# Two tiles for the turned reciprocals, and a new order table for the attention stage

## The chip, the cores and the metric

The kernel is written by hand for one core of one Trainium2 chip. The metric is the time of one execution on the device, in microseconds (us). The engines that the text names are TensorE (PE, with its weight loads shown apart as PEld), VectorE (DVE), ScalarE (ACT), GpSimd (POOL) and SyncE (SP, which here only issues transfers).

## The reference

The program runs cluster attention, then a channel mix, then a token and channel mixer, on 2 batches of 768 positions with 512 features (8 heads of 64), all in float32. Cut to what matters:

```python
# attention, per batch and head: S = 768, D = 64, 16 clusters
q_assign = argmax(q_n @ c_n.T)          # cluster of each query, the same for keys
mask     = q_assign[:, None] == k_assign[None, :]
scores   = where(mask, (q @ k.T) / 8, -1e9)
attn     = exp(scores - rowmax(scores))
out      = (attn / (rowsum(attn) + 1e-9)) @ v
# channel mix: xk, xr are mixes of x with x shifted by one position
x = sigmoid(xr @ w_r) * (relu(xk @ w_k) ** 2 @ w_v)
# mixer
u = x + (relu(x.T @ w_tok1) @ w_tok2).T
out = u + relu(u @ w_ch1) @ w_ch2
```

## The kernel before, in words

**The attention stage** works on 8 pairs, a pair being two heads of one batch. A pair has 12 tasks: two halves of the queries (hf 0 and 1), three blocks of 128 query rows in a half, and the two heads. For a task PE makes the scores (L688, 8 matmuls), DVE takes the row maxima (L696), and ACT takes the exponential from PSUM (L705) and sums its rows on the way. For hf 0 PE turns the tile (L755, two groups of three matmuls), and DVE (L460) or ACT (L462) copies each group to SBUF as ptp. For hf 1 DVE turns 32x32 blocks (L734, into the tile tb), and after the sixth task 16 transfers "ptd<-tb" (L744, 11 issued by SP, 5 by POOL) move the blocks into place. Then PE multiplies by the values (L771, 12 matmuls for a half), and DVE scales the result by the reciprocal row sums and writes it to xT (L780).

**The reciprocals** go a way of their own, once for each half: POOL adds 1e-9 (L711), DVE takes the reciprocal into the tile rsp (L714) and turns it into the tile rst (L717), SP saves rst to DRAM (L721, "rrow<-rst"), and two loads bring it back as one row broadcast over the partitions, rb (L728). There is one rsp and one rst, so the next half's turn waits until the save has read rst.

**The work of the next pair** runs beside this: ACT and POOL split q and k into a high and a low part (L462, L464, L509), PE takes the similarities to the cluster centres (L518, L563), DVE finds the best centre (L568 to L585), and from that a mask is made (L609, L614, L621). Also beside it run five conversions of 128x512 weights into high and low parts (`w_split`): a shift on DVE (L287), two more DVE operations (L291, L297), a comparison (L305), two copies on ACT and a subtraction (L311 on DVE, or on POOL for the gate's weights). At the end the shifted mixes of x for the gate are made (L382, L384, L391, L393), and PE runs 18 gate steps (54 matmuls of L439) between the values' products of the last pairs.

**The order** of all this is not found at run time. Every step above is an `Op` with an engine, a planned duration and what it depends on, and a table of 1141 numbers, `ORDER`, written into the source, says in which order the ops are issued; each engine then runs its own in that order. `ON_VECTOR` says which copies of turned tiles are DVE's, `BANKS` which PSUM bank an op uses. The planner that made the table has a clock for each engine, and a lock for what it counts as using both DVE and POOL at the port that they share: ops marked `two=True` don't overlap there. After the stage comes the dense part (L1159, L1197 and following), whose order is made while the program is built.

Of the kernel before, what the change touches and what calls it, by code (L numbers as in the profile page):

```python
# [9 lines left out]
F32 = mybir.dt.float32  # L10
# [8 lines left out]
P = 128  # L19
# [77 lines left out]
)  # L97
ON_VECTOR = {
    30, 37, 46, 148, 155, 157, 164, 171, 282, 289, 294, 296, 426, 435, 551, 678, 692, 699, 704, 815, 822, 831, 939, 946, 960, 962,
}  # L100
BANKS = (
    "6650647526504652105640246012402641432063254310476306320462046042630254376541063403642020460476307625"
    "6417024704676024024026471602165405264750742062042754065276410632043263204204604260235426543054365406"
    "525062076436720634721064012607654320"
# [26 lines left out]
def cluster_attention_moe_mixer(ctx: ExitStack, tc, q, k, v, cent, mu_k, mu_r, w_k, w_v, w_r, w1, w2, wc1, wc2, out):  # L131
    nc = tc.nc
# [313 lines left out]
    with ExitStack() as actx:  # L446
        vp = actx.enter_context(tc.tile_pool(name="vp", bufs=2))
        ep = actx.enter_context(tc.tile_pool(name="ep", bufs=4))
        ptp = actx.enter_context(tc.tile_pool(name="ptp", bufs=1))
        sml = actx.enter_context(tc.tile_pool(name="sml", bufs=2))  # L450
        dram = actx.enter_context(tc.tile_pool(name="dram", bufs=2, space=bass.MemoryType.DRAM))
        rsp = sml.tile([P, 32], F32, tag="rsp", bufs=1, name="rsp")
        rst = sml.tile([P, 32], F32, tag="rst", bufs=1, name="rst")

        pairs = [(b, p) for b in range(B) for p in range(NPAIR)]
        raws, stks, vts = {}, {}, {}

        def copy(eng, dst, src):
            if eng == "D":
# [1217 lines left out]
```

## Time and profile before

| | |
|---|---|
| median of 3 runs | 603.25 us (603.0 to 604.57) |
| the profiled execution, its own time | 603.43 us |
| span of the profiled execution | 601.6 us |
| PE busy | 591.5 us (98%), 3273 matmuls |
| PE weight loads busy | 489.7 us (81%) |
| DVE busy | 505.2 us (84%), 952 instructions |
| ACT busy | 352.5 us (59%) |
| POOL busy | 129.7 us (22%) |
| granted TensorE clock | 1.00 |

The span is what the trace covers; the execution's own time is 1.8 us longer. Times of single instructions below count from the start of the span. The attention stage fills about the first 218 us of it, the dense part the rest.

### The profile page before, as it was taken

How to read it: one execution, taken by the hardware profiler on the slowest of the kernel's cores; microseconds unless marked ns; L12 is line 12 of the kernel's file. 1: busy time of each engine (PE TensorE's matmuls, PEld its weight loads, DVE VectorE, ACT ScalarE, POOL GpSimd, SP SyncE). 2: the span in 40 equal slices, each digit the busy share in tenths (PEclk: the TensorE clock that was granted, in tenths of full speed). 3: DMA queues.
4: the chain of work that ended last, by engine and by line, in shares of the span. 5: the costliest groups of instructions: out<-in, count | busy, mean ns of one | idle time of the engine just before them, and what ended most of it. 6: DMA issues, size and time to landing. Idle time of an engine off the chain costs nothing.

```text
span 601.6 us, 9577 instructions
## 1 busy us (share of the span) xinstructions
PE 591.5 (98%) x3273; PEld 489.7 (81%) x3273; DVE 505.2 (84%) x952; ACT 352.5 (59%) x661; POOL 129.7 (22%) x182
## 2 busy tenths in 40 slices
PE   8999999999999999999999999999999999999997
PEld 6666767757667668999999998889999998998896
DVE  5999999999999779999579888989889867766634
ACT  4998988988878767967566566134343332222210
POOL 4554644744441750000000000220220000000000
PEclk9999999999999999999999999999999999999999
DMA  8278869888647542343204457245543003233002
GB/s 285 87 207 230 207 199 239 213 266 243 183 133 207 136 155 71 134 127 126 70 2 141 134 184 277 77 133 176 159 122 106 1 1 109 92 124 131 1 0 106
DMA packets 42160, 84.09 MB, mean 140 GB/s; under 512 B 9280, under 2 KB 23104, under 8 KB 42112
## 3 DMA queue, kind: packets, MB, share of 16 engines
q1 hardware_dynamic: 39168, 76.01, 41.3%
q0 software_dynamic: 2944, 7.48, 5.0%
q8 instruction: 26, 0.43, 0.3%
q14 instruction: 22, 0.18, 0.1%
HBM read 51.42 MB, written 8.65 MB: 100 GB/s over the span
## 4 chain that ended last, share of the span: by engine, by line
PE 87%; DVE 7%; issue 2%; DMA 2%; SPq 1%; ACT 1%; POOL 0%; DVEq 0%; POOLq 0%
PE ps L1159 19%; PE ps L1197 18%; PE ps L771 8%; PE ps L1467 8%; PE ps L688 8%; PE ps L1479 7%; PE ps L439 6%; PE ps L755 3%; DVE junk L696 3%; PE ps L1341 3%; PE ps L1253 3%; DVE tb L734 1%; DMA t<-k_dram 1%; SPq L744 1%; PE ps L790 1%
## 5 line engine op out<-in xcount | busy, mean ns | idle before, releaser
L1197 PE MATMUL ps<-wu,hl 128*128 128x512 f32 x486 | 115.2, 391 | 0.0
L1197 PEld LDWEIGHTS ps<-wu,hl 128*128 128x128 f32 x486 | 90.9, 188 | 18.0
L705 ACT ACTIVATE e<-ps,nm 128x768 f32<-128x768 f32 x96 | 86.4, 901 | 15.4 <-DVE junk L696 12.4
L696 DVE TENSOR_SCALAR_CACHE_REDUCE junk<-ps 128x768 bf16<-128x768 f32 x96 | 90.6, 944 | 3.3 <-DVE junk L696 0.9
L1159 PE MATMUL ps<-xmix,wu 128*128 128x384 f32 x384 | 69.2, 335 | 0.0
L1159 PEld LDWEIGHTS ps<-xmix,wu 128*128 128x128 f32 x384 | 67.3, 188 | 1.1
L309 ACT ACTIVATE wu<-g 128x512 fp32r<-128x512 f32 x52 | 32.7, 628 | 47.4 <-DVE g L305 47.2
L1300 POOL DMA_DIRECT2D uperm<-ublk x32 | 16.0, 507 | 203.2 <-DVE ublk L1279 171.6
L688 PE MATMUL ps<-ka,qa 128*128 128x384 f32 x192 | 55.5, 370 | 0.6 <-DVE ptp L460 0.2
L1467 PE MATMUL ps<-wu,hl 128*128 128x512 f32 x216 | 54.7, 393 | 0.0
L1159 PE MATMUL ps<-ut,wu 128*128 128x384 f32 x288 | 52.0, 335 | 0.0
L1159 PEld LDWEIGHTS ps<-ut,wu 128*128 128x128 f32 x288 | 50.5, 188 | 0.9
L688 PE MATMUL ps<-kb,qb 80*128 80x384 f32 x192 | 49.7, 340 | 1.0 <-DVE qb L632 1.0
L1467 PEld LDWEIGHTS ps<-wu,hl 128*128 128x128 f32 x216 | 40.2, 188 | 6.7
L734 DVE STREAM_TRANSPOSE tb<-e 128x768 f32<-128x768 f32 x48 | 44.6, 957 | 0.8 <-DMA t<-q_dram 0.7
L1526 ACT ACTIVATE hl<-t 128x384 fp32r<-128x384 f32 x24 | 12.6, 525 | 55.7 <-DVE t L1522 55.7
L688 PEld LDWEIGHTS ps<-ka,qa 128*128 128x128 f32 x192 | 30.9, 189 | 13.9 <-ACT e L705 6.7
L305 DVE SCALAR_TENSOR_TENSOR g<-wu,g 128x512 f32<-128x512 f32 x52 | 38.7, 746 | 3.9
L1522 DVE TENSOR_TENSOR t<-ps,t 128x384 f32<-128x384 f32 x42 | 22.9, 556 | 22.1 <-PE ps L1479 21.8
L755 PE MATMUL ps<-ident,e 128*128 128x128 f32 x288 | 38.9, 274 | 1.9 <-ACT e L705 1.1
L311 DVE TENSOR_TENSOR wu<-g,wu 128x512 fp32r<-128x512 f32 x48 | 33.1, 690 | 6.4 <-ACT wu L309 5.0
L755 PEld LDWEIGHTS ps<-ident,e 128*128 128x128 f32 x288 | 33.2, 141 | 6.1 <-ACT e L705 1.6
(144 smaller groups left out, 1091.4 us busy)
## 6 DMA issues: line engine op xcount, KB each, us to landing
ptd<-tb SPq DMA_DIRECT2D x88, 144.0 KB, 4.0
wraw<-moe_w_ch_dram SPq DMA_DIRECT2D x24, 512.0 KB, 3.6
t<-q_dram SPq DMA_DIRECT2D x16, 384.0 KB, 4.9
t<-k_dram SPq DMA_DIRECT2D x16, 384.0 KB, 4.5
ptd<-tb POOLq DMA_DIRECT2D x40, 144.0 KB, 4.5
spill<-wu SPq DMA_DIRECT2D x10, 512.0 KB, 3.0
wu<-spill SPq DMA_DIRECT2D x10, 512.0 KB, 4.0
wraw<-moe_w_k_dram SPq DMA_DIRECT2D x9, 512.0 KB, 5.8
```

The source lines that it names most:

```text
L305: nc.vector.scalar_tensor_tensor(out=gf, in0=f32(t[:, 1, :]), scalar=TINY, in1=gf, op0=ALU.is_ge, op1=ALU.mult)
L439: nc.tensor.matmul(gps[b, st][1], xr(xl, c, slice(st * P, (st + 1) * P)), u[:, wl, :], start=(c == 0 and n == 0), stop=(c == KD - 1 and n ...
L688: nc.tensor.matmul(ps[:, nh, 0:HS], x[:, e, c0 : c0 + P], y[:, e, nh * HS : (nh + 1) * HS], start=first, stop=not first,)
L696: nc.vector.tensor_scalar(junk, PS_[t][:, :, 0:HS], -SCALE, None, op0=ALU.mult, op1=ALU.min, accum_out=nm)
L705: nc.scalar.activation(et.rearrange("p (a b) -> p a b", a=2), PS_.pop(t)[:, :, 0:HS], AF.Exp, bias=NM_.pop(t), scale=SCALE, accum_out=ss_[ ...
L734: nc.vector.transpose(out=T_[n][:, :, e, :, i, :].rearrange("p j k q -> p k j q"), in_=E_.pop(t).rearrange("p (k j c) -> p k j c", j=4, c=32),
L755: nc.tensor.transpose(ps[:, kk], E_[t][:, kt * P : (kt + 1) * P], ident)
L771: nc.tensor.matmul(o, vts[n][:, e, kt, :], m, start=(kt == 0), stop=(kt == NT - 1))
L1159: nc.tensor.matmul(ps[:, 0:HS], u[:, wl, c, :], xin(xl, c, sl), start=(n == 0), stop=(n == 11))
L1197: nc.tensor.matmul(accs[st], prev[:, xl, st * P : (st + 1) * P], u[:, wl, :], start=(idx == 1 and n == 0), stop=(idx == nf and n == 2),)
L1467: nc.tensor.matmul(accs[st], self.hl[q][k][:, xl, st * P : (st + 1) * P], u[:, wl, :], start=(left[st] == 2 * np_ - 1 and n == 0), stop=(l ...
L1479: nc.tensor.matmul(ps[:, 0:HS], a(wl, c), b(xl, c), start=(n == 0), stop=(n == 5))
```

## The change

It has three parts. First, a second tile for the turned reciprocals: the halves hf 0 go on using rst, the halves hf 1 use the first 32 columns of csq, a small tile of the start of the program that is now allocated earlier. The rules of the plan follow: a reciprocal comes after the last turn (rsp free) and no longer after the last save, and a turn comes after the save before last. Second, the first step of a weight conversion, the shift, is marked as using the shared port, as the four DVE steps behind it were already. Third, `ORDER`, `ON_VECTOR` (26 entries in both) and `BANKS` are found anew with that.

```diff
-    9, 10, 18, 17, 1051, 1059, 1067, 2, 0, 1, 19, 26, 124, 20, 16, 3, 21, 4, 5, 27, 22, 24, 33, 23, 6, 28, 7, 8, 34, 14, 25, 11, 15, 29, 31, 12, 35,
...
+    9, 10, 18, 17, 1051, 1059, 1067, 2, 0, 1, 19, 26, 124, 20, 16, 3, 21, 27, 4, 22, 28, 24, 5, 33, 6, 25, 7, 29, 1052, 14, 34, 30, 11, 15, 12, 35,
...
-        rst = sml.tile([P, 32], F32, tag="rst", bufs=1, name="rst")
+        csq = sml.tile([P, D], F32, tag="csq", bufs=1, name="csq")
+        rsts = [sml.tile([P, 32], F32, tag="rst", bufs=1, name="rst"), csq[:, 0:32]]
...
         def rturn(n, hf):
-            nc.vector.transpose(out=rst, in_=rsp)
+            nc.vector.transpose(out=rsts[hf], in_=rsp)
...
-            nc.sync.dma_start(out=d.rearrange("r (j q) -> j r q", j=4), in_=rst)
+            nc.sync.dma_start(out=d.rearrange("r (j q) -> j r q", j=4), in_=rsts[hf])
...
-        csq = sml.tile([P, D], F32, tag="csq", bufs=1, name="csq")
...
-            o = rec_[n, hf] = Op("D", 0.12, lambda: recip(n, hf), [o] + list(row_.values())[-1:])
-            o = Op("D", 0.15, lambda: rturn(n, hf), [o])
+            o = rec_[n, hf] = Op("D", 0.12, lambda: recip(n, hf), [o] + rturns[-1:])
+            o = Op("D", 0.15, lambda: rturn(n, hf), [o] + list(row_.values())[-2:-1])
+            rturns.append(o)
```

In the changed kernel the line numbers are one higher from L453 on and two higher behind the attention stage.

**DVE, where the fourth conversion's shift (L287) stood.** This is the preparation of pair 6, which runs beside pair 5's scores; xT_98 holds the second batch's attention output. Before:

```order
L696 TENSOR_SCALAR junk,nm<-ps 128x768
L571 TENSOR_TENSOR ps<-ps,mx 128x384
L576 TENSOR_TENSOR ps<-ps,rank 128x384
L287 TENSOR_SCALAR g<-wraw 128x512
L780 TENSOR_TENSOR xT_98<-ps,rb 128x384
L582 TENSOR_REDUCE m_1818<-ps 128x24
L585 TENSOR_TENSOR oh<-ps,m_1818 128x24x16
L696 TENSOR_SCALAR junk,nm<-ps 128x768
```

After, from the same subtraction of the maxima (now L572) to the shift's new place:

```order
L572 TENSOR_TENSOR ps<-ps,mx 128x384
L577 TENSOR_TENSOR ps<-ps,rank 128x384
L583 TENSOR_REDUCE m_1807<-ps 128x24
L781 TENSOR_TENSOR xT_98<-ps,rb 128x384
L718 STREAM_TRANSPOSE csq<-rsp 128x32
...
L586 TENSOR_TENSOR oh<-ps,m_1807 128x24x16
...
L697 TENSOR_SCALAR junk,nm<-ps 128x768 x2
L287 TENSOR_SCALAR g<-wraw 128x512
L697 TENSOR_SCALAR junk,nm<-ps 128x768
```

The shift has left the place ahead of the scaling to xT (L780) and stands five row maxima later, between the row maxima of tasks 67 and 68 (tasks are numbered through the pairs, 12 to each).

**PE, at the first values' product of pair 3's second half** (`ptd,v_1173`, whose moves end at about 121 us). Before:

```order
L755 MATMUL ps<-ident,e 128x128 x9
L609 LDWEIGHTS oh
...
L609 MATMUL ps<-identb,oh 128x128
L688 MATMUL ps<-ka_1117,qa_1115 128x384 x2
L688 MATMUL ps<-kb_1118,qb_1116 128x384 x2
L771 MATMUL ps<-ptd,v_1173 64x384 x4
L688 MATMUL ps<-ka_1117,qa_1115 128x384 x2
```

After:

```order
L689 MATMUL ps<-kb_1104,qb_1102 128x384 x2
L756 MATMUL ps<-ident,e 128x128 x3
L772 MATMUL ps<-ptd,v_1174 64x384 x4
L689 MATMUL ps<-ka_1103,qa_1101 128x384 x2
L689 MATMUL ps<-kb_1104,qb_1102 128x384 x2
L689 MATMUL ps<-ka_1103,qa_1101 128x384 x2
L689 MATMUL ps<-kb_1104,qb_1102 128x384 x2
L756 MATMUL ps<-ident,e 128x128 x3
```

The first matmuls that need the moved blocks have the same work ahead of them but for the last three matmuls that turn pair 4's first-half tiles (L755, now L756): these stand behind them, after two further score tasks.

**DVE, at the first turn of pair 4's second half** (L734, into the tile tb), which must wait until pair 3's moves have read that tile. Before:

```order
L305 SCALAR_TENSOR_TENSOR g<-wu,g 128x512
L717 STREAM_TRANSPOSE rst<-rsp 128x32
L696 TENSOR_SCALAR junk,nm<-ps 128x768
L734 STREAM_TRANSPOSE tb<-e 128x6x4x32
L696 TENSOR_SCALAR junk,nm<-ps 128x768
L291 SCALAR_TENSOR_TENSOR g<-wraw,g 128x512
```

After:

```order
L305 SCALAR_TENSOR_TENSOR g<-wu,g 128x512
L718 STREAM_TRANSPOSE rst<-rsp 128x32
L697 TENSOR_SCALAR junk,nm<-ps 128x768
L291 SCALAR_TENSOR_TENSOR g<-wraw,g 128x512
L697 TENSOR_SCALAR junk,nm<-ps 128x768
L735 STREAM_TRANSPOSE tb<-e 128x6x4x32
```

A conversion step (L291) and one more row maximum have moved ahead of the turn.

At the end of the stage three more things move, told here in words. On DVE the last turn of pair 6 stands behind two more row maxima (L696), a conversion step (L291) and a scaling (L780). On PE the products of pair 6's second half are now the last ahead of the 54 gate matmuls, behind three steps of pair 7's first half that stood after them. And the last of pair 7's first-half steps, two matmuls, has moved behind those gates.

## Rows read from the trace of the kernel before

**Rows 1.** The profile's page: span and busy time of each engine.

```profile
span 601.6 us, 9577 instructions
...
PE 591.5 (98%) x3273; PEld 489.7 (81%) x3273; DVE 505.2 (84%) x952; ACT 352.5 (59%) x661; POOL 129.7 (22%) x182
```

**Rows 2.** Stretches: from:to, us, PE, PEld, DVE, ACT, POOL, clock, DMA, GB/s.

```profile
60.00:110.00 50.00, 50.00 (x354) 35.49 (x340) 48.97 (x100) 43.63 (x85) 29.34 (x31) 1.00 0.78 210
110.00:165.00 55.00, 53.23 (x364) 38.31 (x361) 53.23 (x110) 47.29 (x96) 25.83 (x31) 1.00 0.84 231
```

**Rows 3.** Chain that ended last, 105 to 220 us: start, us.

```profile
118.14 3.10 DMA t<-q_dram
...
135.70 1.82 DVE g L287
...
141.40 0.66 PE ps L755 x6
...
169.11 2.14 PE ps L771 x12
...
195.40 5.96 PE ps L771 x36
...
213.86 4.02 PE ps L771 x24
```

**Rows 4.** Timeline of DVE, 135.2 to 138.5 us: start, us, instruction.

```profile
135.70 1.82 DVE L287 TENSOR_SCALAR g<-wraw 128x512 uint32<-128x512 uint32 x1
137.44 0.55 DVE L780 TENSOR_TENSOR xT<-ps,rb 128x384 f32<-128x384 f32 x1
```

**Rows 5.** Timeline of POOL around the same time, 135 to 138 us.

```profile
135.41 1.83 POOL L509 TENSOR_TENSOR qb<-t,qa 64x768 fp32r<-64x768 f32 x1
```

**Rows 6.** All runs of the line L287: shortest, median and longest in ns.

```profile
L287 DVE TENSOR_SCALAR g<-wraw x5: 383/418/1819, 19.9 to 175.1; 128x512 uint32<-128x512 uint32 x5
```

**Rows 7.** PE's timeline at two of its waits, about 121 and 138 us.

```profile
121.27 1.51 PE L771 MATMUL ps<-ptd,v 128*64 128x384 f32 x8 [0.68 <-ACT ptp L462]
...
138.04 0.88 PE L755 MATMUL ps<-ident,e 128*128 128x128 f32 x6 [0.81 <-DVE xT L780]
```

**Rows 8.** DVE groups, 14-201 us: count | busy, mean ns | idle.

```profile
L696 DVE TENSOR_SCALAR_CACHE_REDUCE junk<-ps 128x768 bf16<-128x768 f32 x96 | 90.6, 944 | 3.3 <-DVE junk L696 0.9 <-ACT e L705 0.5 <-PE ps L563 0.4
L734 DVE STREAM_TRANSPOSE tb<-e 128x768 f32<-128x768 f32 x48 | 44.6, 957 | 0.8 <-DMA t<-q_dram 0.7
...
L780 DVE TENSOR_TENSOR xT<-ps,rb 128x384 f32<-128x384 f32 x13 | 6.9, 545 | 0.0
...
L291 DVE SCALAR_TENSOR_TENSOR g<-wraw,g 128x512 uint32<-128x512 uint32 x5 | 3.4, 687 | 0.0
```

**Rows 9.** DVE's waits, 0 to 218 us: us in total, times, longest.

```profile
DVE rst L717 <- DMA rrow<-rst: 2.4, 1, 2.4
...
DVE junk L696 <- DVE junk L696: 0.9, 6, 0.2
```

**Rows 10.** SP's queue: moves of pairs 2, 6 and 7, and the last save.

```profile
84.63 0.54 SPq L744 DMA_DIRECT2D ptd<-tb  x1
...
90.38 5.83 SPq L744 DMA_DIRECT2D ptd<-tb  x5
...
180.27 8.98 SPq L744 DMA_DIRECT2D ptd<-tb  x11
...
201.68 4.69 SPq L744 DMA_DIRECT2D ptd<-tb  x6
...
207.10 3.29 SPq L744 DMA_DIRECT2D ptd<-tb  x5
...
211.72 0.59 SPq L721 DMA_DIRECT2D rrow<-rst  x1
```

**Rows 11.** ACT's timeline at the end of the stage.

```profile
209.60 1.28 ACT L1035 ACT_TABLE_LOAD   x1
...
215.53 1.58 ACT L391 ACTIVATE xmix<-t 128x768 fp32r<-128x768 f32 x2 [1.23 <-DVE t L384]
```

More of the change, by code (lines that the diff above doesn't have):

```diff
@@ L56 @@
 ORDER = (
[40 rows of a table removed]
[40 rows of a table added]
 )
 ON_VECTOR = {
-    30, 37, 46, 148, 155, 157, 164, 171, 282, 289, 294, 296, 426, 435, 551, 678, 692, 699, 704, 815, 822, 831, 939, 946, 960, 962,
+    23, 37, 58, 155, 162, 169, 176, 185, 280, 287, 289, 412, 419, 426, 553, 574, 685, 697, 706, 815, 822, 829, 953, 955, 960, 967,
 }
 BANKS = (
-    "6650647526504652105640246012402641432063254310476306320462046042630254376541063403642020460476307625"
-    "6417024704676024024026471602165405264750742062042754065276410632043263204204604260235426543054365406"
-    "525062076436720634721064012607654320"
+    "6650345240654204765274560642604200746271065410362402670427024027564065264507625651420640260425046534"
+    "2150642052364306046043261204120621034076247072042614072106540346210540645402602764076432610342163243"
+    "063046210476206546324032634027654210"
 )
@@ L881, in cluster_attention_moe_mixer @@
         prep, score_, max_, exp_, turn_, tp_, ev_, move_, pv_, xe_, parts, load_, mask_dma, load_v_ = ({} for _ in range(14))
+        rturns = []
         row_, rec_, simt_, mask_, re_ = ({} for _ in range(5))
@@ L1020, in cluster_attention_moe_mixer @@
             back = ("G", 1.4, True) if i < KD else ("D", 0.62, True)
-            conv.append(steps(w_split, [("D", 0.36, False), ("D", 0.62, True), ("A", 0.56, False), ("D", 0.62, True),
+            conv.append(steps(w_split, [("D", 0.36, True), ("D", 0.62, True), ("A", 0.56, False), ("D", 0.62, True),
                                         ("D", 0.62, True), ("A", 0.55, False), back],
```

78 rows, old and new, of the table ORDER are left out of this document.

## The prediction

> **What bounds the kernel now.** Read the page first: PE is busy for 591.5 of 601.6 us [rows 1]. There is little for any change here to win, and a microsecond counts only where PE stands still. So the next view is the busy time by stretch. In 60 to 110 us PE shows no idle time, in 110 to 165 us it shows 1.77 us (55.00 less 53.23), and DVE is idle for as little there, 1.77 us [rows 2]. Two engines share the bound in this stage. The chain of waits says which of them ends last: from about 113 to 166 us it runs through DVE for the most part, and from 169.11 us on it lies on PE without a break, to the end of the stage and beyond [rows 3]. A microsecond that DVE saves between 110 and 165 us can come through; one that it saves after 169 us can't, unless PE waits for it.
>
> **The shift.** The five shifts of the weight conversions take 0.38 to 0.42 us, but one took 1.82 us [rows 6]. That one started at 135.70 us, 0.29 us after POOL had started a subtraction of 1.83 us (135.41 to 137.24), and it ended at 137.52 [rows 4, 5]: a shift that begins inside a POOL operation lasts as long as POOL does and then its own 0.28 us. Right behind it in DVE's queue stood the scaling to xT (L780, at 137.44), which frees the PSUM bank that PE's next turned tile needed. PE stood still for 0.81 us and named that scaling as what it waited for [rows 4, 7]. In the changed order the shift stands between two row maxima, after the preparation of pair 6, where no POOL subtraction stands beside it in the order. It should take 0.38 us, so DVE gains 1.82 less 0.38 = 1.44 us. The bounds of what comes through: nothing, if PE's other work takes up the room; 0.81 us, if only the wait counts that PE shows; 1.44 us, if DVE sets the pace after it too. I take 1.44, since the chain goes on through DVE for 30 us after this place, so that what DVE saves reaches the moment at which PE takes over (169.11). The four other shifts have nothing to give back.
>
> The Trainium skill (SBUF — State Buffer, "Who interferes with whom") says that VectorE and GpSimd have one port pair as an exclusive lock and that whoever issues first keeps it for the whole instruction. The trace agrees: by that rule alone the shift would have ended about 137.24 + 0.38 = 137.62 us, and it ended at 137.52. The same page ("SBUF: two separate sides") warns that a transfer issued by GpSimd can't have its descriptors written while VectorE holds the pair, with 620 ns alone against 3100 ns. The third conversion's shift now follows pair 3's last reciprocal, beside POOL's issues of pair 3's moves; an estimate from that page would add up to 2.5 us to five of the 16 moves there, and the sum would become about 602.5 us. No row of before shows a shift at such a place, and its 0.38 us are too short to hold a move that long, so I leave it out.
>
> **The wait for pair 3's moves.** At 121.27 us PE stood still for 0.68 us ahead of the first product of pair 3's second half [rows 7]. The row names a copy by ACT, but at the same moment DVE's wait for the tile tb ended, 0.7 us, by the landing of the last of those moves, 3.10 us after the issue [rows 3, 8]. The change touches both engines here. On DVE a conversion step (L291, 0.69 us) and a row maximum (0.94 us) [rows 8] have moved ahead of the turn that waits; that is 1.63 us of work for a wait of 0.7, so the wait should be gone and DVE gains 0.7. On PE three turning matmuls have moved from ahead of the product to behind it. Six take 0.66 us [rows 3], so PE comes to its wait 0.33 us sooner, waits that much longer, and has the 0.33 us still to do: a loss of 0.33. The bounds are therefore a loss of 0.33, if PE sets the pace at this place, and a gain of 0.70, if DVE does. I take both together, a gain of 0.37, since the chain passes through both.
>
> **Small items.** Where a row maximum follows directly on another, DVE waits 0.15 us for it (0.9 us in 6 waits) [rows 9]. Counting pairs in the order, there are 14 before and 15 after: +0.15 us, between 0 and 0.15. DVE has the same number of operations to the end of the stage, 26 copies of turned tiles among them, so nothing else is added there.
>
> **The second tile.** It removes one wait that the profile shows: the last turn waits 2.4 us for the save of the half before [rows 9], at the very end of the stage. PE is then in the 54 gate matmuls, which begin after 201.36 us and end at 213.86 [rows 3], with 90 more behind the last products, so the wait is hidden and its removal is worth 0. If the gates did not cover it, it would be worth up to 2.4 us. The tile brings a wait of its own: the Sigmoid's warm-up on ACT writes a column of csq, so the load of its table (209.60 us before) now waits for the save of pair 7's second half, issued at 211.72 for 0.59 us [rows 10, 11]. With a landing as long as the 3.10 us of the moves it goes to about 215.4, then 1.28 us for the load and the warm-up behind it: 216.9. Queued behind it on ACT are two parts of the gate's mix, which started at 215.53 us [rows 11]; they would be some 1.4 us late. PE needs them only in gate steps behind the first of those 90 matmuls, so I cost it at 0; without that cover it is 1.4 us.
>
> **The sum.** 603.43 us (the profiled execution) less 1.44 less 0.37 plus 0.15 = 601.77. That execution was 0.18 us above the median of 603.25, so I say 601.6 us.
>
> **The rivals.**
>
> *Nothing shows.* PE is busy for 53.23 of 55.00 us in the stretch [rows 2]; an earlier DVE may only meet PE's own work, or the next transfer that lands at its own time. Then only the small items count, and the time is 603.2 us, no more than 0.1 off before. For it speaks that PE lost only 0.81 us at the shift; against it that the chain is DVE's for the 30 us behind.
>
> *More than the sum.* PE's loads of weights are busy only for 35.49 of 50.00 us even where PE shows no idle time, and for 38.31 of 55 us behind that [rows 2]. If PE is thus never the bound ahead of 169 us, every wait of DVE comes through when it is closed. Beside the terms of the sum these are 0.5 us for exponentials and 0.4 for the centres [rows 8], and PE's 0.33 at pair 3's moves would cost nothing: 601.6 less 1.23 is 600.4 us. The order of the first 60 us is new too, and I give the better case 0.4 us more room for it, to 600.0. Against it: the new order can close them, but nothing says that it closes all. The Trainium skill (Perfetto Trace Analysis, "Identifying the Most-Contended Engine") holds busy matmuls for a poor measure and the share of weight loads for a better one; by it this rival is the case here.
>
> *Slower: the moves of pairs 6 and 7.* The last turn of pair 6 now stands behind two more row maxima (0.94 each), a conversion step (0.69) and a scaling (0.55) [rows 8], 3.1 us of work, and its moves start by that much later: 180.27 + 3.1 - 1.4 = 182.0 us. SP issues them in 9.0 us, and 3.1 us later they have landed [rows 3, 10], at 194.1, before the turns of pair 7, which write into the same tile, would start (six of 0.96, ending about 200.2, which is the 201.68 of their moves in before less 1.44). But pair 2's moves took from 84.63 to 96.21, 11.6 us [rows 10]. At that pace pair 6's land at 196.7, pair 7's turns end at 202.5, and pair 7's moves (8.7 us before, from 201.68 to 210.39) land at 214.3, or at 217.2 at the slow pace. PE needs them about 212.7 us, when the gates (213.86 less 1.81 by the sum's two gains) and the moved step of pair 7 (a sixth of the 4.02 us that six steps take) are over. It would wait 1.6 to 4.5 us: 603.2 to 606.1, middle 604.6 us. It decides from a delay of some 1.7 us beyond what I expect at that place. Against it: at the pace that these moves had in before there are 0.7 us to spare.
>
> **How the numbers follow.** Chances: the sum 0.45 (its own range 601.1 to 602.6, from a shift worth 0.81 with nothing gained at the moves to a shift worth 1.44 with 0.70 there and no row maximum more), nothing shows 0.22, more than the sum 0.22, slower 0.11. The range of 8 in 10 reaches from 600.0, where the better rival lies, to 603.9, past the one that shows nothing, and leaves out most of the slower one. A measurement of this kernel can tell about 0.3% (1.8 us) from no change, so faster means below 601.44. Some 0.19 of the sum's 0.45 lies there, and nearly all of the better rival: 0.40. Slower means above 605.06: 0.07. The rest is 0.53.
>
> **What would show it.** Right: every shift ahead of 201 us at 0.38 to 0.42 us, no 0.81 us wait of PE for L781, and the chain on PE for good some 1.5 us earlier than 169.11; the 54 gate matmuls start near 199 us (201.36 less 1.81 and the moved step); the 2.4 us wait of L718 gone with no effect. The step on the second tile is wrong if PE waits for ACT after the gates. The whole is wrong if a new wait for moves (L735 or L772 behind "ptd<-tb") of a microsecond or more shows, or if PE's losses in the first 60 us, where the order is new as well and which I take as unchanged, differ by more than a microsecond.

## The result, and the profile after

The changed kernel takes 608.46 us (median of 4 runs, 607.33 to 609.16) against 603.49 us (603.0 to 604.57) for the kernel before: a ratio of 1.0083, with a 95% interval of 1.0067 to 1.0099, or 5.0 us more. The forecast was 601.6 us, with a range of 600.0 to 603.9. The profiled execution of the changed kernel took 607.33 us with a span of 605.5, 3.9 us more than before. It is the fastest of the four, so its trace accounts for 3.9 of the 5.0 us; two of the other three had a lower mean granted clock (0.996 and 0.997, against 0.999), which matters further down.

The same first views as before. The page; the stretches, first the one from 20 us on in the kernel before, which [rows 2] does not have, then four of the changed kernel; and PE's timeline at each place behind 14 us where it stood still for over a microsecond:

```profile
span 605.5 us, 9555 instructions
...
PE 591.8 (98%) x3273; PEld 490.1 (81%) x3273; DVE 504.4 (83%) x952; ACT 352.5 (58%) x661; POOL 130.7 (22%) x182
```

```profile
20.00:60.00 40.00, 39.01 (x269) 26.69 (x276) 39.04 (x81) 36.13 (x71) 22.63 (x23) 1.00 0.58 165
```

```profile
20.00:60.00 40.00, 37.47 (x251) 26.55 (x245) 37.76 (x78) 33.26 (x67) 21.35 (x20) 1.00 0.56 162
60.00:110.00 50.00, 48.06 (x341) 32.74 (x337) 47.31 (x96) 42.32 (x85) 26.39 (x28) 1.00 0.73 199
110.00:165.00 55.00, 52.91 (x359) 37.60 (x357) 53.60 (x108) 47.63 (x94) 29.54 (x35) 1.00 0.81 229
165.00:201.00 36.00, 35.60 (x230) 26.49 (x230) 34.66 (x71) 29.28 (x61) 10.39 (x13) 1.00 0.60 166
```

```profile
27.48 0.51 PE L610 MATMUL ps<-identb,oh 128*128 128x128 bf16 x6 [1.51 <-DVE oh L586]
...
102.73 0.54 PE L772 MATMUL ps<-ptd,v 128*64 128x384 f32 x2 [1.94 <-DMA ptd<-tb]
...
143.71 0.61 PE L689 MATMUL ps<-ka,qa 128*128 128x384 f32 x2 [1.97 <-DVE oh L586]
```

PE does the same work (591.8 us, 591.5 before). In 20 to 60 us it is busy for 37.47 us (39.01 before). In 60 to 110 us, where it had no idle time [rows 2], it now has 1.94. The two waits of [rows 7] are gone, and three longer ones stand at other places. How the delay builds up can be read from one matmul that both kernels have, the first of a task's scores:

| first matmul of | before | after | later by |
|---|---|---|---|
| task 27's scores | 64.27 us | 65.51 us | 1.24 us |
| task 48's scores | 106.79 | 109.94 | 3.15 |
| task 57's scores | 122.70 | 125.28 | 2.58 |
| task 65's scores | 140.44 | 143.71 | 3.27 |
| task 84's scores | 177.28 | 181.00 | 3.72 |
| pair 7's second products | 213.79 | 217.74 | 3.95 |

Behind that point nothing is added: the span is 3.9 us longer. So 1.24 us are lost at the start, 1.9 between 65 and 110 us, 0.7 between tasks 57 and 65, where the shift should have brought 1.4, and another 0.7 behind that; 0.6 is gained between tasks 48 and 57. The shift itself did what was forecast. All runs of its line; then the line of 1 - mu in the kernel before; then DVE's and POOL's timelines at the wait of 143.7 us:

```profile
L287 DVE TENSOR_SCALAR g<-wraw x5: 384/423/434, 16.9 to 179.2; 128x512 uint32<-128x512 uint32 x5
```

```profile
L1001 DVE TENSOR_SCALAR omu<-mu x1: 160/160/160, 69.7 to 69.7; 128x8 f32<-128x8 f32 x1
```

```profile
140.74 2.46 DVE L1003 TENSOR_SCALAR omu<-mu 128x8 f32<-128x8 f32 x1
143.11 0.54 DVE L586 TENSOR_TENSOR oh<-ps,m 128x384 bf16<-128x384 f32 x1
```

```profile
139.35 1.98 POOL L745 DMA_DIRECT2D ptd<-tb  x4
141.34 1.82 POOL L510 TENSOR_TENSOR ka<-t,ka 64x768 fp32r<-64x768 f32 x1
```

No shift is over 0.44 us any more [rows 6]. But a very small instruction, 1 - mu over 128x8 elements for the channel mix (L1003; L1001 and 0.16 us in the kernel before), now takes 2.46 us. It ends 0.04 us after POOL's subtraction; the long shift of [rows 4, 5] ended 0.28 us after POOL's. Behind it stands the one-hot of the best centres (L586), which frees the bank that PE's next scores need. The 1 - mu stands at the very place whose order is shown ahead of the prediction, among the lines left out between L718 and L586, and its `Op` carries no `two=True`: it is one more step that the planner doesn't count.

The wait at 102.7 us comes from pair 2's moves. SP's timeline, and the piece of the chain of waits that ends it:

```profile
87.40 0.54 SPq L745 DMA_DIRECT2D ptd<-tb  x1
...
92.75 4.96 SPq L745 DMA_DIRECT2D ptd<-tb  x5
```

```profile
97.21 4.96 DMA ptd<-tb
102.17 0.56 issue
102.73 1.51 PE ps L772 x8
```

They start at 87.40 us, 2.8 later than in [rows 10], and the last lands at 102.2; before, it landed at about 98.1 (issued at 95.62, 2.5 us). So 2.8 of some 4 us are the late start. The rest is that the moves are longer under way, as the medians from issue to landing between 84 and 104 us show (the last number of a row; before, then after):

```profile
ptd<-tb SPq DMA_DIRECT2D x11, 144.0 KB, 3.9
ptd<-tb POOLq DMA_DIRECT2D x5, 144.0 KB, 5.4
```

```profile
ptd<-tb SPq DMA_DIRECT2D x11, 144.0 KB, 7.0
ptd<-tb POOLq DMA_DIRECT2D x5, 144.0 KB, 7.0
```

The start waits for two things, which these rows of DVE and of PE show:

```profile
85.81 0.97 DVE L735 STREAM_TRANSPOSE tb<-e 128x768 f32<-128x768 f32 x1
```

```profile
86.54 0.81 PE L772 MATMUL ps<-ptd,v 128*64 128x384 f32 x4
```

The first is pair 2's last turn into tb, which the new order puts behind one more row maximum. The second is the last product of pair 1's second half, which must have read the tile ptd before it is written again; the new order puts it behind three scores and two products of pair 2.

### The profile page after: what moved, and what is told of

It is laid out like the page before. It is cut to its first block, busy times and chain, and to the rows that moved or that the text cites. A ratio compares the mean times of both kernels' runs of the same rounds, so it can differ in the third digit from the quotient of the medians.

```text
span 605.5 us, 9555 instructions
## 1 busy us (share of the span) xinstructions
PE 591.8 (98%) x3273; PEld 490.1 (81%) x3273; DVE 504.4 (83%) x952; ACT 352.5 (58%) x661; POOL 130.7 (22%) x182
## 4 chain that ended last, share of the span: by engine, by line
PE 87%; DVE 5%; DMA 3%; issue 2%; SPq 1%; ACT 1%; POOL 0%; DVEq 0%; POOLq 0%; ACTq 0%
PE ps L1161 19%; PE ps L1199 18%; PE ps L772 9%; PE ps L689 8%; PE ps L1469 8%; PE ps L1481 7%; PE ps L439 5%; PE ps L756 3%; PE ps L1343 3%; PE ps L1255 3%; DVE junk L697 2%; DMA ptd<-tb 2%; SPq L745 1%; DMA t<-k_dram 1%; PE ps L791 1%
## 5 line engine op out<-in xcount | busy, mean ns | idle before, releaser
L735 DVE STREAM_TRANSPOSE tb<-e 128x768 f32<-128x768 f32 x48 | 44.6, 958 | 1.5 <-DMA ptd<-tb 0.7
L756 PE MATMUL ps<-ident,e 128*128 128x128 f32 x288 | 39.8, 274 | 0.5 <-ACT e L706 0.4
L305 DVE SCALAR_TENSOR_TENSOR g<-wu,g 128x512 f32<-128x512 f32 x52 | 35.8, 689 | 4.0
L291 DVE SCALAR_TENSOR_TENSOR g<-wraw,g 128x512 uint32<-128x512 uint32 x52 | 37.2, 717 | 0.9
```

The costliest lines, as they stand in the source:

```text
L291: nc.vector.scalar_tensor_tensor(out=g, in0=high, scalar=0xC0000000, in1=g, op0=ALU.bitwise_and, op1=ALU.bitwise_or)
L305: nc.vector.scalar_tensor_tensor(out=gf, in0=f32(t[:, 1, :]), scalar=TINY, in1=gf, op0=ALU.is_ge, op1=ALU.mult)
L735: nc.vector.transpose(out=T_[n][:, :, e, :, i, :].rearrange("p j k q -> p k j q"), in_=E_.pop(t).rearrange("p (k j c) -> p k j c", j=4, c=32),
L756: nc.tensor.transpose(ps[:, kk], E_[t][:, kt * P : (kt + 1) * P], ident)
```

## The experiments

Each kernel ran in turns with the kernel before on the same chip; ratios are to that, with 95% intervals. An edit of the table is shown by the rows that move.

**The shift alone.** The kernel before, with the one shift at its new place:

```diff
 L576 TENSOR_TENSOR ps<-ps,rank 128x384
-L287 TENSOR_SCALAR g<-wraw 128x512
 L780 TENSOR_TENSOR xT_98<-ps,rb 128x384
...
 L696 TENSOR_SCALAR junk,nm<-ps 128x768
+L287 TENSOR_SCALAR g<-wraw 128x512
 L696 TENSOR_SCALAR junk,nm<-ps 128x768
```

> The kernel before with one instruction moved in the table: the fourth conversion's shift (L287, 1.82 us, behind POOL) goes to between the row maxima of tasks 67 and 68, as in the changed kernel. The prediction's step: 0.38 us, PE's 0.81 us wait at 138 us goes and the time falls by 1.44 us to 602.0. Rival B (PE and DVE share the bound): only PE's wait or less is returned, 602.6 to 603.4.

Measured: 602.04 us against 603.28, ratio 0.9971 (0.9961 to 0.9981): 1.24 us less by the medians, 1.75 by the ratio (1.15 to 2.35). The stretch around the place:

```profile
110.00:165.00 55.00, 54.29 (x376) 39.49 (x373) 53.35 (x113) 48.80 (x99) 26.70 (x34) 1.00 0.86 237
```

PE is busy 1.06 us longer in the same 55 us [rows 2]. The step of the prediction holds: more came back than the 0.81 us of PE's own wait, and the 1.44 lies within the interval. This is also the fastest kernel of the study.

**The second tile alone.** The changed code with the order, the vector copies and the banks of before:

```diff
-    9, 10, 18, 17, 1051, 1059, 1067, 2, 0, 1, 19, 26, 124, 20, 16, 3, 21, 27, 4, 22, 28, 24, 5, 33, 6, 25, 7, 29, 1052, 14, 34, 30, 11, 15, 12, 35,
+    9, 10, 18, 17, 1051, 1059, 1067, 2, 0, 1, 19, 26, 124, 20, 16, 3, 21, 4, 5, 27, 22, 24, 33, 23, 6, 28, 7, 8, 34, 14, 25, 11, 15, 29, 31, 12, 35,
...
```

> The two tiles and the rules alone: the changed kernel's code with the order, the vector copies and the banks of the kernel before. Theory A (the loss is all in the new order): 603.4 us, within 0.4 of the kernel before; the 2.4 us wait of the last turn for the save goes without effect. Rival C (the second tile costs by itself, by the wait of ACT's table load for the last save): 1 us or more above the kernel before, with PE waiting in the gates behind the last products.

Measured: 606.8 us against 603.28, ratio 1.0047 (1.003 to 1.0064). Theory A, as written for this run, was wrong; what rival C named is there. ACT's timeline at the end of the stage, and PE's in the gates:

```profile
215.63 1.28 ACT L1037 ACT_TABLE_LOAD   x1 [5.62 <-DMA rrow<-csq]
```

```profile
223.11 3.01 PE L439 MATMUL ps<-wu,xmix 128*128 128x512 f32 x12 [0.21 <-ACT sg L1113]
227.80 13.90 PE L439 MATMUL ps<-wu,xmix 128*128 128x512 f32 x60 [1.68 <-ACT sg L1113]
```

ACT stands still for 5.62 us before the Sigmoid's table load, since the warm-up writes a column that the last save reads, and PE then waits for the Sigmoid's results. To tell this wait from any other price of the tile, the warm-up was moved to a column that no save reads:

```diff
-        Op("A", 1.4, lambda: nc.scalar.activation(csq[:, 0:1], half, AF.Sigmoid), [exp_[NTASK * NP - 1]])
+        Op("A", 1.4, lambda: nc.scalar.activation(csq[:, 32:33], half, AF.Sigmoid), [exp_[NTASK * NP - 1]])
```

> The two tiles with the order of before, as in the run that took 606.8 us, but the Sigmoid's warm-up writes column 32 of csq, which no save reads, in place of column 0. Theory C' (what the second tile costs under the old order is ACT's wait for the last save, 5.62 us, with PE's 1.9 us and more behind it): the wait is gone and the time is that of the kernel before, 603.3 within 0.5. Rival (the two tiles cost in another way, the rules or the saves): it stays above 605.5.

Measured: 603.47 us against 603.47, ratio 1.0004 (0.9995 to 1.0014). So the two tiles and their rules are worth nothing that the measurement can tell, and the shared column costs 2.6 us by the ratios under the old order. In the trace of the changed kernel it costs next to nothing: there the new order puts other work of ACT ahead of the table load:

```profile
214.96 1.75 ACT L382 ACTIVATE t<-xT,omu 128x768 f32<-128x768 f32 x2
218.27 1.28 ACT L1037 ACT_TABLE_LOAD   x1 [1.55 <-DMA rrow<-csq]
```

PE has no wait of a microsecond behind it there, and from pair 7's second products to the end of the 90 gate matmuls behind them it takes 24.6 us, as in the kernel before. No run has the new order with the other column, so this part is read from the trace alone. The loss of the changed kernel lies in the order.

**1 - mu beside POOL.** The changed kernel with that instruction earlier:

```diff
 L586 TENSOR_TENSOR oh<-ps,m_1048 128x24x16
+L1003 TENSOR_SCALAR omu<-mu 128x8
 L697 TENSOR_SCALAR junk,nm<-ps 128x768
...
 L697 TENSOR_SCALAR junk,nm<-ps 128x768
-L1003 TENSOR_SCALAR omu<-mu 128x8
 L586 TENSOR_TENSOR oh<-ps,m_1807 128x24x16
```

> The changed kernel with one DVE instruction moved in the table: 1 - mu (L1003, 128x8, 2.46 us in the changed kernel's trace against 0.16 before) goes from behind row maximum 63 to behind aoh3 (the one-hot of pair 3's centres, near 75.7 us), where POOL stands idle from 74.4 to 83.1 us. Theory A (DVE sets the pace there and the instruction waited for POOL at the shared port): it takes 0.16 us again, PE's 1.97 us wait at 143.7 us goes, and the time falls by 2.3 us, from 608.5 to about 606.2. Rival B (PE and DVE share the bound, another wait takes its place): the instruction is short again but the time stays within 0.7 us of 608.5.

Measured: 606.01 us, ratio 1.0038 (1.0025 to 1.0051); the changed kernel had 1.0083, so 2.7 us came back by the ratios, whose intervals lie apart. PE's wait at that place is gone, and the instruction took its 0.16 us:

```profile
L1003 DVE TENSOR_SCALAR omu<-mu x1: 163/163/163, 76.0 to 76.0; 128x8 f32<-128x8 f32 x1
```

Theory A holds. A second run moved it by one place only, to where POOL issues transfers:

```diff
+L1003 TENSOR_SCALAR omu<-mu 128x8
 L697 TENSOR_SCALAR junk,nm<-ps 128x768
-L1003 TENSOR_SCALAR omu<-mu 128x8
 L586 TENSOR_TENSOR oh<-ps,m_1807 128x24x16
```

> The changed kernel with 1 - mu one place earlier, ahead of row maximum 63, where it begins near 139.8 us while POOL issues four transfers (139.35 to 141.33 us) and not yet the subtraction behind them. Theory A1 (only POOL's arithmetic holds the port): 0.16 us, and the time falls by about 2.3 us to 606.2. Theory A2 (POOL's issue of a transfer holds DVE's instruction up as well): it takes until 141.3 us or, if the next subtraction comes first again, 143.2: 1.5 to 3.4 us, and the time stays at 607.5 to 609.5.

Measured: 605.24 us, ratio 1.0043 (1.0023 to 1.0064). DVE's and POOL's timelines:

```profile
139.94 0.16 DVE L1003 TENSOR_SCALAR omu<-mu 128x8 f32<-128x8 f32 x1
```

```profile
139.60 1.98 POOL L745 DMA_DIRECT2D ptd<-tb  x4
141.59 1.84 POOL L510 TENSOR_TENSOR ka<-t,ka 64x768 fp32r<-64x768 f32 x1
```

A1 holds for this place: 0.34 us into the issues of the same four transfers, nothing holds it up, and the time returns (2.4 us by the ratios). One row maximum later it had waited for the whole subtraction.

**Pair 2's moves.** The changed kernel with the last turn of pair 2 and the last product of pair 1 earlier. DVE's rows, then PE's:

```diff
-L735 STREAM_TRANSPOSE tb<-e 128x6x4x32 x3
-L697 TENSOR_SCALAR junk,nm<-ps 128x768
-L735 STREAM_TRANSPOSE tb<-e 128x6x4x32
+L735 STREAM_TRANSPOSE tb<-e 128x6x4x32 x4
+L697 TENSOR_SCALAR junk,nm<-ps 128x768
...
-L772 MATMUL ps<-ptd,v_270 64x384 x10
+L772 MATMUL ps<-ptd,v_270 64x384 x12
 L689 MATMUL ps<-ka_839,qa_837 128x384 x2
...
-L772 MATMUL ps<-ptd,v_270 64x384 x2
```

> The changed kernel with pair 2's last turn ahead of row maximum 36 and the last product of pair 1's second half ahead of score 36, so that both things that its moves wait for (86.78 and 87.07 us) end about 0.9 us and 4 us earlier. Theory A (late moves of pair 2 cost what PE and DVE wait for them): the moves start at about 86 instead of 87.4 us, PE's wait of 1.94 us at 102.7 us shrinks to some 0.5, DVE's waits of 0.69 and 0.65 us go, and the time falls by about 1.3 us to 607.2. Rival B (the moves land when the transfer engines let them, whenever they start; or another wait takes the place): landing stays near 102.2 us or the time within 0.5 us of 608.5.

Measured: 606.2 us, ratio 1.0041 (1.0027 to 1.0055). By the ratios 2.5 us came back, more than expected. In its trace the moves start at 84.94 us, the last lands at 98.9, and the product has no wait ahead of it; DVE's two waits behind it went too. SP's row, then PE's:

```profile
84.94 0.54 SPq L745 DMA_DIRECT2D ptd<-tb  x1
```

```profile
99.61 1.46 PE L772 MATMUL ps<-ptd,v 128*64 128x384 f32 x8
```

By task 48 this trace is 2.5 us ahead of the changed kernel's (107.48 against 109.94). It shows one thing more. The 1 - mu is still at its late place, and PE waits 1.99 us for it, until 141.34 us. Directly behind that wait the granted clock is at its lower level, 1.2 GHz, and it is back at 2.4 GHz from 145 us on:

```profile
142.00:145.00 3.00, 3.00 (x13) 2.90 (x12) 2.15 (x6) 2.42 (x5) 0.00 (x0) 0.50 1.02 268
```

The same matmuls that took 2.17 us behind the same wait in the changed kernel's trace (143.71 to 145.88), where the clock stayed up, take 3.75 here: 1.6 us more. So a wait of PE can cost more than its own length, in some executions and not in others. This is a candidate for the 1.1 us that the median of the changed kernel lies above its profiled execution; those executions have no trace, so it is not shown.

Then both edits in one kernel:

> The changed kernel with the two edits that worked alone, 1 - mu at 76 us and pair 2's moves earlier. Theory A (they add up): 608.5 less 2.45 less 2.26 = 603.75 us, about the kernel before. Rival B (they overlap, since the first places PE's wait where the second would have): 605 us or more.

Measured: 603.6 us against 603.76, ratio 1.0003 (0.9989 to 1.0017). They add up: of the 5.0 us nothing is left that the measurement can tell.

**The start.** The first 236 operations of the table, the same ones in both, in the order of before (its beginning stands in the diff of the second tile's run) and with that kernel's vector copies, the rest as changed and the banks of the rest given out anew:

> The changed kernel with the first 236 operations of the table (to about 55 us, the same operations in both tables) in the order of the kernel before, with that kernel's vector copies, and banks given out anew from there. Theory A: the changed kernel lost 1.24 us by there (PE waits 1.51 us for the first mask at 27.5 us, DVE idles afterwards), and that comes back: 608.5 less 1.2 = 607.2 us. Rival B (later waits stand where they stood, at transfers): the time stays within 0.5 us of 608.5.

Measured: 608.81 us, ratio 1.0092 (1.0067 to 1.0117). Nothing came back. The trace shows how: the first matmul of task 21's scores is 1.97 us earlier than in the changed kernel (51.98 against 53.95), that of task 24 is 0.18 later (61.91 against 61.73). Between them ACT waits:

```profile
60.05 0.84 ACT L463 ACTIVATE ka<-t 128x768 fp32r<-128x768 f32 x1 [3.45 <-DMA t<-k_dram]
60.80 0.88 ACT L706 ACTIVATE e<-ps,nm 128x768 f32<-128x768 f32 x1
```

The new order splits pair 3's k for the second head first, whose load is the last of four, and queues an exponential behind it; the order of before takes the first head's. SP issues that load at 51.85 us, 1.3 earlier than in the changed kernel (53.14), and it lands no earlier: ACT's row starts at 60.05, in the changed kernel at 59.84. In the changed kernel this wait is 1.10 us and lies behind the start's loss, so each hides the other. The next run put the exponential ahead of the split:

```diff
-L706 ACTIVATE e,ss<-ps,nm 128x768 x2
+L706 ACTIVATE e,ss<-ps,nm 128x768 x3
 L463 ACTIVATE ka_839<-t 128x768
-L706 ACTIVATE e,ss<-ps,nm 128x768
 L463 ACTIVATE qa_837<-t 128x768
```

> The run with the start of before, which gained 2 us by 52 us and had lost it again by 62, with one more edit: on ACT the split of pair 3's k for the second head, which waited 3.45 us for its load, goes behind the exponential of task 23 that stood behind it. Theory D (that wait for the load ate the start's gain): the exponential no longer waits, and the time falls by 1.2 us or more, to 607.3 or less. Rival E (the next transfer holds in its turn: POOL issues pair 1's last moves behind four other operations, and pair 2's first turn waits for them): the time stays within 0.5 us of 608.5, and DVE's wait at that turn, 0.53 us in that run, grows to 1.5 us or more.

Measured: 608.44 us, ratio 1.0078 (1.0058 to 1.0098). The time is rival E's. In the trace 1.1 us of the start's gain are still there at task 27 (64.43 against 65.51 us); behind that, PE and DVE wait for pair 1's moves. PE's row, DVE's at the first turn of pair 2, and a stretch with the clock:

```profile
81.38 0.91 PE L772 MATMUL ps<-ptd,v 128*64 128x384 f32 x2 [2.98 <-DMA rrow<-rst]
```

```profile
81.27 0.98 DVE L735 STREAM_TRANSPOSE tb<-e 128x768 f32<-128x768 f32 x1 [3.69 <-issue]
```

```profile
81.00:86.00 5.00, 4.62 (x16) 2.06 (x18) 4.73 (x8) 2.86 (x5) 0.49 (x1) 0.50 0.16 46
```

This profiled execution, 611.09 us, is the slowest of the six (the others took 607.11 to 608.97). In it the clock fell to its lower level at about 80 us, while PE waited, and stayed there until about 86.6, so the size of its waits need not be that of the others.

The turn must wait until pair 1's moves have read tb. In the changed kernel POOL issues the last of them at 73.89 us, behind four other operations, where the kernel before was done with them at 68.07. POOL's last move of pair 1 there, and the turn that follows:

```profile
73.89 0.56 POOL L745 DMA_DIRECT2D ptd<-tb  x1
```

```profile
78.84 0.98 DVE L735 STREAM_TRANSPOSE tb<-e 128x768 f32<-128x768 f32 x1 [0.17 <-issue]
```

POOL's row in the run with the exponential earlier:

```profile
72.93 0.55 POOL L745 DMA_DIRECT2D ptd<-tb  x1
```

So rival E names the right transfer, but its late issue is not all. Here the move is issued 0.96 us earlier than in the changed kernel and lands 2.4 us later, 8.3 us after its issue (4.9 in the changed kernel). SP issues the first of the next four loads of q and k at 72.13 us, ahead of that move; in the changed kernel it does so at 73.95, behind it. That the move then shares the transfer engines with those loads fits; no run tells it apart from the place of the issue.

**All together.** First the start with the two edits that worked:

> The three edits together: the start in the order of before, pair 2's last turn and pair 1's last product earlier, and 1 - mu at 76 us. Theory A (three losses at three places that add up, and the shift's gain of 1.2 to 1.4 us left over): 608.5 less 1.2, less 2.3, less 2.4 = 602.5 us, a little under the kernel before. Rival B (PE and DVE share the bound, so losses overlap): the three return less together than apart, 603.5 us or more.

Measured: 604.47 us against 603.47, ratio 1.0021 (1.0008 to 1.0034). The time is rival B's: with the earlier start it is no better than without it (1.0003). What holds it is not a shared bound but a transfer: the turn at 81.36 us waits 2.44 us for pair 1's moves. (The banks of this run were given out anew as well; they differ from those of the run with the start alone.) With that put right too, by the exponential ahead of the split and POOL's last two moves of pair 1 ahead of its other work (POOL's rows):

```diff
-L745 DMA ptd<-tb 32x1152
+L745 DMA ptd<-tb 32x1152 x3
 L465 CAST kb_840<-t 64x768
 L510 TENSOR_TENSOR ka_839<-t,ka_839 64x768
 L510 TENSOR_TENSOR qb_838<-t,qa_837 64x768
-L745 DMA ptd<-tb 32x1152
 L712 TENSOR_SCALAR ss<-ss 128x6
-L745 DMA ptd<-tb 32x1152
```

> All edits together: the start of before, the exponential of task 23 ahead of the split of k, POOL's last two moves of pair 1 ahead of its other work there, pair 2's moves earlier, 1 - mu at 76 us. Theory A with D and E (each wait for a transfer held the next, and all are now out of the way): 1.2 to 2 us below the run with the two edits, 602 to 602.5 us, at or under the 602.0 of the kernel before with the shift moved. Rival B: no better than the run with the two edits.

Measured: 603.24 us against 603.76, ratio 0.9993 (0.9981 to 1.0005), 0.1% under the run with two edits, with intervals that overlap, so a gain is not shown. In its profiled execution (601.85 us) the waits are gone:

```profile
20.00:60.00 40.00, 38.94 (x262) 26.27 (x260) 38.97 (x80) 35.43 (x69) 21.48 (x21) 1.00 0.56 165
60.00:110.00 50.00, 50.00 (x352) 35.06 (x338) 48.60 (x101) 43.98 (x87) 29.18 (x32) 1.00 0.75 213
110.00:165.00 55.00, 54.70 (x378) 39.72 (x374) 53.33 (x112) 48.98 (x99) 27.92 (x32) 1.00 0.87 238
165.00:201.00 36.00, 36.00 (x222) 24.44 (x221) 35.12 (x66) 28.24 (x57) 12.54 (x15) 1.00 0.48 130
```

Its median doesn't show as much as this one execution, so that the expected 602 to 602.5 us are not reached stays unexplained. The kernel before with its one shift moved remains the better one (0.9971).

## Why the prediction was wrong

**The shift.** Right in mechanism and in size: 1.44 us forecast; the run with it alone gave 1.24 by the medians and 1.75 by the ratio (1.15 to 2.35). The choice between PE's wait (0.81) and all that DVE saves (1.44) was right as well: DVE set the pace there.

**The wait for pair 3's moves.** Right in direction, too small. From task 53's first score to task 57's took 8.75 us before and takes 7.53 in the changed kernel; 0.33 of it is the turning that now comes behind, so about 0.9 us were gained, against 0.37 forecast with an upper bound of 0.70. But there everything comes 2.6 to 3.8 us later, so the moves had more time as well; how much of it is the order's is not told apart. One reading beneath this step was wrong. The row of 3.10 us [rows 3] names a load of q, issued at 118.14 us behind the last moves, and not a move; SP's queue before:

```profile
115.36 2.67 SPq L744 DMA_DIRECT2D ptd<-tb  x4
118.14 0.51 SPq L472 DMA_DIRECT2D t<-q_dram  x1
```

So 3.10 us is no time of a move from issue to landing, though the prediction uses it as one for pairs 6 and 7 and for the last save. It is not what made the forecast miss.

**"Nothing else is added there."** This step failed, by 2.3 us in the trace and 2.7 by the run that undid it. The count of DVE's operations was the same in both orders, and I took equal counts for equal time. What an instruction costs depends on what POOL does beside it, and 1 - mu, at 0.16 us too small to look at, took 2.46. The prediction had the mechanism in hand, a DVE instruction that lasts as long as POOL's, and used it for the shift only.

**The first 60 us "which I take as unchanged".** Not as assumed: PE loses 1.54 us more there, and the scores of task 27 begin 1.24 later, which is over the microsecond that the prediction set as a sign of being wrong. What it cost in the end is not shown. Given back by itself it returned nothing, since a load, and behind it pair 1's last moves, landed no sooner; with these out of the way too, 0.6 us came back by the ratios, within the noise. The run with two edits, which keeps the shift's gain and the start's loss, ends where the kernel before does, so about as much as the shift brought is still lost in it; the start is the nearest candidate.

**The slower rival.** It had the right kind of mechanism, moves that start late and land behind the moment at which PE wants them, and looked at pairs 6 and 7. There it did not bite: in the changed kernel pair 6's moves start at 187.13 us, the turns of pair 7 run from 200.30 without a wait, and PE has none. It stood at pair 2. The prediction took that pair's 11.6 us only as a pace for others, and did not ask when pair 2's own moves begin in the new order. That cost 1.9 us in the trace and 2.5 by the run that undid it, which with the 1 - mu turned a gain into a loss. These two steps are what failed: with both undone, nothing of the 5.0 us is left.

**The second tile.** "I cost it at 0" was right for the changed kernel, but not for the reason given. Without cover the price was set at 1.4 us; under the old order, where ACT reaches the table load sooner, it was 2.6 by the ratios, and the gates did not hide it. The table load itself came when the prediction said (215.63 us there, 215.4 forecast). The chain behind it was cut short: the two parts of the mix began 4.5 us late (220.03 against 215.53), not 1.4, because another step of ACT (L382), which DVE needs first, stood behind the load as well. What hid it in the changed kernel is, by its trace, the new place of the warm-up.

**What bounds the kernel.** Right: a microsecond counts where PE stands still, and behind task 65's scores no more than 0.7 us is added, and none of it comes back.

## What to carry to other kernels

In an order that is found anew, check every VectorE instruction of a kind that was seen to wait for GpSimd (here `tensor_scalar` from SBUF to SBUF) against what GpSimd does at that time, the smallest ones too, as they are the ones that nobody counts. Follow each transfer back to the last thing that its start waits for, in the new order, for every repetition of the pattern and not just for the one that the chain of waits happens to show. And a wait that is taken away upstream of a transfer brings nothing until the transfer itself lands sooner: look at the queue that issues it, and at which other transfers are issued ahead of it.

## What the runs showed of the hardware

A DVE instruction of 0.16 us took 2.46 to 2.48 us in four traces (the changed kernel, the run with pair 2's moves earlier, the run with the start of before, and that run with the exponential earlier), each time from about 1.4 us into POOL's issue of four transfers until 0.02 to 0.04 us after the subtraction behind them; 0.34 us into the same issues it took 0.16. The Trainium skill (SBUF — State Buffer, "Who interferes with whom") says that whichever of VectorE and GpSimd issues first gets the port pair. Read by the starts in the records, the trace does not agree here: the small instruction began 0.6 us before the subtraction's record and still waited for its end. Whether the subtraction or the last of the issues already held the port then, no run tells apart. Not every DVE instruction from SBUF to SBUF waits like this: in the changed kernel three turns (L735, 82.34 to 85.03 us) kept their 0.9 us each beside a subtraction of POOL (83.09 to 84.93).

How long a move takes to land is not a constant of the move: the last of pair 2's landed 4.96 us after its issue in the changed kernel and 2.5 before, and the last of pair 1's 4.9 us after it in the changed kernel and 8.3 in the run with the exponential earlier.

In the attention stage the granted clock fell to 1.2 GHz in two traces, with a wait of PE of 1.99 us (pair 2's moves earlier) and one of 2.98 us (the exponential earlier); it did not fall at PE's waits of 1.94 and 1.97 us in the changed kernel's trace. While it was down, matmuls that had taken 2.17 us took 3.75.
